# Attention scores of two heads: one zero-padded matmul over the whole array, or two on halves of its rows

## The chip, the cores and the metric

The kernel runs on one core of a Trainium2 chip. The metric is the device time of one execution in microseconds (us); the median of three runs of the kernel before is 1846.34 us (1845.67 to 1846.72). The engines are TensorE (PE in the rows, PEld its weight loads), VectorE (DVE), ScalarE (ACT), GpSimd (POOL) and SyncE (SP), which issues the transfers.

## The reference

Attention over pooled keys and values feeds two layers of matmuls. Batch 8, 8 heads, 576 positions, head size 64; keys and values are averaged over 8 positions, so each head has 72 keys.

```python
k_p = k.reshape(B, H, Sp, pool, D).mean(axis=3)        # 72 keys of 64
v_p = v.reshape(B, H, Sp, pool, D).mean(axis=3)
scores = scale * np.matmul(q, k_p.transpose(0, 1, 3, 2))
scores = scores - np.max(scores, axis=-1, keepdims=True)
attn = np.exp(scores)
attn = attn / (np.sum(attn, axis=-1, keepdims=True) + 1e-09)
x = np.matmul(attn, v_p)                               # to 4608 x 512
h = x @ w_in;  g = h * sigmoid(1.702 * h);  x = g @ w_out      # 512 -> 2048 -> 512
a = x @ w_a;   b = x @ w_b;  out = (a * b) @ w_out2            # 512 -> 1536 -> 512
```

## The kernel before

The 4608 positions are 36 query tiles of 128 (`u`), and four query tiles are a block of 512 (`j`, nine blocks). A batch has 4.5 query tiles, so four of the 36 lie across two batches; `pieces(u)` cuts such a tile into two halves of 64 positions. The two big layers run in four passes over the blocks; each float32 operand is split into a high and a low part, and `mm3` makes three matmuls of 128x512 of each product (lines 130 to 132, and 415 to 417 for the last matmul). They are most of the work: some 7300 of the 8592 MATMULs in the trace.

The attention of later blocks is spread between the big matmuls of the first pass. A query tile goes through these steps:

- `stage_b1(u, half)`, once for each half of the heads: the scores of two pairs of heads into one bank `sc` of PSUM (line 224), the negated maximum of each row on VectorE (line 231), four exponentials with their sums on ScalarE (line 234).
- `stage_b2(u)`: normalises the weights `at` on VectorE (line 248).
- `stage_c(u)`: eight transposes of `at` through PE (`pt`, line 256), copied to `aT` by ScalarE.
- `stage_d(u)`: attention times values, two heads into the two halves of the partitions of `px` (line 269), then the split into `xhi` and `xlo`.

A pair of heads stands in one `q` tile: 64 rows for the first head, 64 for the second. The keys stand in `kbd`, 128 rows and, for each pair, 144 columns: the first head's keys in rows 0 to 63 and columns 0 to 71, the second's in rows 64 to 127 and columns 72 to 143, zeros elsewhere (GpSimd, line 160). One matmul of 128 rows and 144 columns then gives the scores of both heads side by side. `sum_k` sums the raw keys on VectorE, and `to_kbd` scales them into place with two ScalarE instructions (lines 191 and 192).

PSUM has eight banks here: four in the pool `acc` for the sums of the big layers, and four in the pool `ps`, which `h`, `ab`, `sc`, `pt` and `px` share. The order on each engine is made by a scheduler that takes the code's order as its input; `spread` puts each attention step behind a step of the big layers, and `in_order` holds the steps of the start behind the newest VectorE instruction. In the trace a float32 matmul of the code is two MATMULs, each with its own weight load; a matmul whose output goes to 64 partitions of PSUM takes half of the array's columns (`px`, and `sc` of the four tiles across two batches).

Of the kernel before, what the change touches and what calls it, by code (L numbers as in the profile page):

```python
# [9 lines left out]
F32 = mybir.dt.float32  # L10
# [14 lines left out]
def tile_kernel(ctx, tc, q, k, v, w_in, w_out, w_a, w_b, w_o2, out):  # L25
# [13 lines left out]
    nc = tc.nc  # L39
    P = 128  # L40
    NU, _, NP, _ = q.shape
    B, SP, H, D, _ = v.shape
# [19 lines left out]
    ps = ctx.enter_context(tc.tile_pool(name="ps", bufs=4, space=bass.MemoryType.PSUM))  # L62
# [7 lines left out]
    def vec(made):  # L70
        newest[0] = made.ins
        return made
# [82 lines left out]

    at = ExitStack()
    ap_ = at.enter_context(tc.tile_pool(name="ap", bufs=1))
    kbd = [ap_.tile([P, NP, 2 * SP], F32, name=f"kbd{i}") for i in range(2)]
    for t in kbd:
        nc.gpsimd.memset(t, 0.0)  # L160

    q_t, ks_t, vs_t, at_t, atT_t, kraw_t, vraw_t = {}, {}, {}, {}, {}, {}, {}

    def pieces(u):

        done = 0
        while done < P:
            b, s = divmod(u * P + done, S)
            n = min(P - done, S - s)
            yield done, n, b  # L170
            done += n

    def load_q(u, t=None):
        q_t[u] = ap_.tile([P, NP, P], F32, tag="q", name="q", bufs=2) if t is None else t
        nc.sync.dma_start(out=q_t[u], in_=q[u])
# [8 lines left out]

    scale = 1.0 / (POOL * D ** 0.5)

    def to_kbd(b, half, ks):


        cs = slice(2 * half, 2 * half + 2)  # L190
        nc.scalar.mul(out=kbd[b % 2][0:D, cs, 0:SP], in_=ks[0:D], mul=scale)
        nc.scalar.mul(out=kbd[b % 2][D:P, cs, SP:2 * SP], in_=ks[D:P], mul=scale)

    def sum_k(b, half):
        ks = ap_.tile([P, 2, SP], F32, tag="ks", name="ks", bufs=1)
        raw = kraw_t.pop((b, half)).rearrange("p c (s r) -> p c s r", r=POOL)
        vec(nc.vector.tensor_reduce(out=ks, in_=raw, op=ALU.add, axis=AX.X))
        to_kbd(b, half, ks)

    def load_v(b, h, n, raw=None):  # L200
        if raw is None:
# [9 lines left out]
    def stage_b1(u, half):  # L211
        qT = q_t[u]
        if half == 0:
            at_t[u] = (
                ap_.tile([P, H, SP], F32, tag="at", name="at", bufs=2),
                ap_.tile([P, H], F32, tag="mx", name="mx", bufs=2),
                ap_.tile([P, H], F32, tag="sm", name="sm", bufs=2),
            )
        a, mx, sm = at_t[u]
        sc = ps.tile([P, H // 2, SP], F32, tag="ps", name="sc")  # L220
        for c in range(2):
            pair = 2 * half + c
            for o, n, b in pieces(u):
                nc.tensor.matmul(  # L224
                    out=sc[o:o + n, 2 * c:2 * c + 2, :].rearrange("p h k -> p (h k)"),
                    lhsT=qT[:, pair, o:o + n],
                    rhs=kbd[b % 2][:, pair, :],
                    start=True, stop=True,
                )
        hs = slice(half * (H // 2), (half + 1) * (H // 2))  # L230
        vec(nc.vector.tensor_reduce(out=mx[:, hs], in_=sc, op=ALU.max, axis=AX.X, negate=True))
        for c in range(H // 2):
            h = half * (H // 2) + c
            nc.scalar.activation(
                out=a[:, h, :], in_=sc[:, c, :], func=AF.Exp, bias=mx[:, h:h + 1],
                accum_out=sm[:, h:h + 1],
            )
        if half == 1:
            q_t.pop(u)
            if UB <= u + 2 < NU:  # L240
                load_q(u + 2)

# [43 lines left out]
    def slot(t, lo, hi):  # L286

        todo = [
            (t, op(stage_b1, t, 0)), (t - 1, op(stage_b2, t - 1)), (t - 2, op(stage_d, t - 2)),
            (t, op(stage_b1, t, 1)), (t - 1, op(stage_c, t - 1)),  # L290
        ]
        return [o for u, o in todo if lo <= u < hi]
# [4 lines left out]
    for b in range(2, B):  # L297
        u0 = b * S // P
        for t, ops in (
            (u0 - 5, [op(load_k, b, 0)]), (u0 - 4, [op(sum_k, b, 0), op(load_k, b, 1), op(load_v, b, 0, V)]),  # L300
            (u0 - 3, [op(sum_k, b, 1), op(load_v, b, V, V)]),
            (u0 - 2, [op(sum_v, b, 0, V), op(load_v, b, 2 * V, V)]),
            (u0 - 1, [op(sum_v, b, V, V), op(load_v, b, 3 * V, V)]),
            (u0, [op(sum_v, b, 2 * V, V)]), (u0 + 1, [op(sum_v, b, 3 * V, V)]),
        ):
            later[t] += ops
# [189 lines left out]
    for i in range(1, 4):  # L496
        fs = passes[i][1]
        for j in range(NB):
            n = place[i, j, fs[0]]
# [74 lines left out]
    def b1(u):  # L574
        return [op(stage_b1, u, half) for half in range(2)]
# [7 lines left out]

    c0, c1 = make_parts((1, 0)), make_parts((1, 1))
    in_order(op(sum_k, 0, 0), op(sum_k, 0, 1), b1(0)[0], c0[0], b1(0)[1], b1(1)[0], c0[1], b1(1)[1])
    in_order(op(sum_v, 0, 0, half_v), b2(0), op(sum_v, 0, half_v, half_v), b2(1), *b1(2))
    in_order(c0[2], cd(0), b1(3)[0], c0[3], cd(1), b1(3)[1], b2(2), c1[0], b2(3), c1[1], cd(2), c1[2], cd(3), c1[3])
# [5 lines left out]
    hs = {}  # L593
# [87 lines left out]
```

## Time and profile before

| | |
|---|---|
| median of three runs | 1846.34 us |
| the profiled execution | 1848.59 us |
| its span, first to last instruction | 1846.8 us |
| mean granted TensorE clock | 0.986 |
| busy: PE, VectorE, ScalarE | 1807.4, 843.7, 549.4 us |
| score MATMULs, busy | 320, 55.3 us (40.4 + 8.3 + 6.6) |
| `px` MATMULs, busy | 640, 45.5 us (40.4 + 5.1) |

Busy times of PE are unions over overlapping instructions: a MATMUL's listed duration runs to the modelled end of its last column, while the next has long begun. What one costs in a stream is therefore the step from its start to the next start, which the timeline gives. The attention ends at about 436 us; after that PE runs the big layers alone.

### The profile page before, as it was taken

What the parts mean: (1) busy time and instruction counts of PE and PEld (TensorE: products, weight loads), DVE (VectorE), ACT (ScalarE), POOL (GpSimd) and SP (SyncE); (2) the same over time, 40 slices, a digit from 0 to 9 for tenths busy, and PEclk for the clock granted to TensorE, in tenths of its full rate; (3) what the DMA queues carried; (4) which work ended last, traced back from release to release, by engine and by line L of the source; (5) the groups of instructions that cost most, each with busy time, mean ns of one, the idle gap of its engine ahead of it and who ended that gap; (6) DMA issues with size and microseconds to landing.
All of it is one profiled execution on the core that took longest, in us unless ns stands there. A gap on an engine that the chain in (4) does not pass through costs nothing.

```text
span 1846.8 us, 21557 instructions
## 1 busy us (share of the span) xinstructions
PE 1807.4 (98%) x8592; PEld 1487.3 (81%) x8592; DVE 843.7 (46%) x1440; ACT 549.4 (30%) x1373; POOL 1.7 (0%) x8
## 2 busy tenths in 40 slices
PE   5799999999999999999999999999999999999998
PEld 4668888888888888888888888888888888888887
DVE  6886767655744444445444445456212221221222
ACT  5555555553322222223222222222111111111111
POOL 0000000000000000000000000000000000000000
PEclk7899999999999999999999999999999999999999
DMA  9263454325333222333223433432211210220200
GB/s 295 105 215 140 170 162 145 128 80 196 147 114 126 91 103 83 123 126 137 103 92 137 171 125 121 153 114 92 91 39 53 92 68 24 92 91 12 80 24 23
DMA packets 58613, 206.92 MB, mean 112 GB/s; under 512 B 6576, under 2 KB 6576, under 8 KB 46704
## 3 DMA queue, kind: packets, MB, share of 16 engines
q1 hardware_dynamic: 58512, 205.55, 31.4%
q8 instruction: 67, 1.10, 0.2%
q14 instruction: 34, 0.28, 0.0%
HBM read 139.46 MB, written 66.06 MB: 111 GB/s over the span
## 4 chain that ended last, share of the span: by engine, by line
PE 95%; DVE 3%; ACT 1%; DMA 1%; issue 0%; DVEq 0%; ACTq 0%
PE ab L130 11%; PE ab L131 11%; PE ab L132 11%; PE h L130 7%; PE h L131 7%; PE h L132 7%; PE acc L130 7%; PE acc L131 7%; PE acc L132 7%; PE acc L415 5%; PE acc L416 5%; PE acc L417 5%; PE px L269 2%; PE sc L224 2%; PE pt L256 2%; DVE vs L209 1%
## 5 line engine op out<-in xcount | busy, mean ns | idle before, releaser
L130 PE MATMUL ab<-xhi,w 128*128 128x512 f32 x864 | 336.1, 389 | 0.0
L131 PE MATMUL ab<-xlo,w 128*128 128x512 f32 x864 | 336.1, 389 | 0.0
L132 PE MATMUL ab<-xhi,w 128*128 128x512 f32 x864 | 336.1, 389 | 0.0
L403 DVE TENSOR_TENSOR c<-c,ab 128x512 f32<-128x512 f32 x108 | 74.3, 688 | 529.5 <-PE ab L132 526.7
L130 PE MATMUL h<-xhi,w 128*128 128x512 f32 x576 | 227.5, 396 | 0.7 <-ACT xhi L85 0.7
L131 PE MATMUL acc<-glo,w 128*128 128x512 f32 x576 | 227.2, 394 | 0.0
L131 PE MATMUL h<-xlo,w 128*128 128x512 f32 x576 | 226.4, 393 | 0.0
L132 PE MATMUL h<-xhi,w 128*128 128x512 f32 x576 | 226.2, 393 | 0.0
L132 PE MATMUL acc<-ghi,w 128*128 128x512 f32 x576 | 225.0, 391 | 0.0
L375 DVE SCALAR_TENSOR_TENSOR g<-g,h 128x512 f32<-128x512 f32 x144 | 98.6, 685 | 232.7 <-ACT g L372 232.2
L130 PE MATMUL acc<-ghi,w 128*128 128x512 f32 x576 | 188.7, 400 | 2.8 <-ACT ghi L376 1.9
L132 PEld LDWEIGHTS ab<-xhi,w 128*128 128x128 f32 x864 | 162.2, 188 | 33.8
L130 PEld LDWEIGHTS ab<-xhi,w 128*128 128x128 f32 x864 | 162.2, 188 | 33.7
L131 PEld LDWEIGHTS ab<-xlo,w 128*128 128x128 f32 x864 | 162.2, 188 | 33.6
L372 ACT ACTIVATE g<-h 128x512 f32<-128x512 f32 x144 | 86.1, 598 | 339.8 <-PE h L132 330.0
L402 ACT COPY c<-ab 128x512 f32<-128x512 f32 x108 | 63.6, 589 | 356.9 <-PE ab L132 356.9
L415 PE MATMUL acc<-w,chi 128*128 128x512 f32 x432 | 168.0, 389 | 0.0
L416 PE MATMUL acc<-w,chi 128*128 128x512 f32 x432 | 168.0, 389 | 0.0
L417 PE MATMUL acc<-w,clo 128*128 128x512 f32 x432 | 167.6, 389 | 0.0
L85 ACT CAST chi<-c 128x512 fp32r<-128x512 f32 x108 | 66.9, 620 | 288.8 <-DVE c L403 288.8
L130 PEld LDWEIGHTS h<-xhi,w 128*128 128x128 f32 x576 | 109.4, 190 | 24.1 <-ACT xhi L85 1.1
L131 PEld LDWEIGHTS h<-xlo,w 128*128 128x128 f32 x576 | 109.6, 190 | 23.4 <-issue 0.4
(61 smaller groups left out, 2067.7 us busy)
## 6 DMA issues: line engine op xcount, KB each, us to landing
part<-ys SPq DMA_DIRECT2D x72, 256.0 KB
part<-part SPq DMA_DIRECT2D x18, 1024.0 KB
xhi<-yd SPq DMA_DIRECT2D x18, 1024.0 KB
xlo<-yd SPq DMA_DIRECT2D x18, 1024.0 KB
xd<-xhi SPq DMA_DIRECT2D x9, 1024.0 KB
xd<-xlo SPq DMA_DIRECT2D x9, 1024.0 KB
xhi<-xd SPq DMA_DIRECT2D x9, 1024.0 KB
xlo<-xd SPq DMA_DIRECT2D x9, 1024.0 KB
```

The source lines that it names most:

```text
L85: nc.scalar.copy(out=hi, in_=src)
L130: nc.tensor.matmul(out=o, lhsT=whi, rhs=xhi, start=first, stop=False)
L131: nc.tensor.matmul(out=o, lhsT=whi, rhs=xlo, start=False, stop=False)
L132: nc.tensor.matmul(out=o, lhsT=wlo, rhs=xhi, start=False, stop=last)
L224: nc.tensor.matmul(out=sc[o:o + n, 2 * c:2 * c + 2, :].rearrange("p h k -> p (h k)"), lhsT=qT[:, pair, o:o + n], rhs=kbd[b % 2][:, pair, : ...
L372: nc.scalar.activation(out=g, in_=hps, func=AF.Tanh, scale=0.5 * 1.702)
L375: made = vec(nc.vector.scalar_tensor_tensor(out=g, in0=g, scalar=1.0, in1=hps, op0=ALU.add, op1=ALU.mult))
L402: nc.scalar.copy(out=cc, in_=pab[0])
L403: made = nc.vector.tensor_tensor(out=cc, in0=cc, in1=pab[1], op=ALU.mult)
L415: nc.tensor.matmul(out=o, lhsT=chi[:, cs], rhs=whi, start=first, stop=False)
L416: nc.tensor.matmul(out=o, lhsT=chi[:, cs], rhs=wlo, start=False, stop=False)
L417: nc.tensor.matmul(out=o, lhsT=clo[:, cs], rhs=whi, start=False, stop=last)
```

## The change

The keys lose their zeros: `kT` holds 128 rows and 72 columns for each pair, the first head's keys in rows 0 to 63, the second's in rows 64 to 127, in the same columns. One ScalarE instruction of 128 rows writes what two of 64 rows did, and GpSimd's zero fill goes. The scores of a pair are two matmuls of 64 rows and 72 columns: one reads rows 0 to 63 of `q` and `kT`, the other rows 64 to 127. They go into two banks: `sc_t[u][0]` takes the even heads and `sc_t[u][1]` the odd ones. All scores of a query tile are now made in `stage_b1(u, 0)`, so both banks are taken there; the second call works on the second bank. A call's maximum and four exponentials are for every second head.

```diff
-    kbd = [ap_.tile([P, NP, 2 * SP], F32, name=f"kbd{i}") for i in range(2)]
-    for t in kbd:
-        nc.gpsimd.memset(t, 0.0)
+    kT = [ap_.tile([P, NP, SP], F32, name=f"kT{i}") for i in range(2)]
...
-    def to_kbd(b, half, ks):
-        cs = slice(2 * half, 2 * half + 2)
-        nc.scalar.mul(out=kbd[b % 2][0:D, cs, 0:SP], in_=ks[0:D], mul=scale)
-        nc.scalar.mul(out=kbd[b % 2][D:P, cs, SP:2 * SP], in_=ks[D:P], mul=scale)
+    def to_kT(b, half, ks):
+        nc.scalar.mul(out=kT[b % 2][:, 2 * half:2 * half + 2, :], in_=ks, mul=scale)
...
+            sc_t[u] = [ps.tile([P, H // 2, SP], F32, tag="ps", name="sc") for _ in range(2)]
+            for pair in range(NP):
+                for o, n, b in pieces(u):
+                    for e in range(2):
+                        r = slice(e * D, (e + 1) * D)
+                        nc.tensor.matmul(
+                            out=sc_t[u][e][o:o + n, pair, :], lhsT=qT[r, pair, o:o + n],
+                            rhs=kT[b % 2][r, pair, :], start=True, stop=True,
+                        )
         a, mx, sm = at_t[u]
-        sc = ps.tile([P, H // 2, SP], F32, tag="ps", name="sc")
-        for c in range(2):
-            pair = 2 * half + c
-            for o, n, b in pieces(u):
-                nc.tensor.matmul(
-                    out=sc[o:o + n, 2 * c:2 * c + 2, :].rearrange("p h k -> p (h k)"),
-                    lhsT=qT[:, pair, o:o + n],
-                    rhs=kbd[b % 2][:, pair, :],
-                    start=True, stop=True,
-                )
-        hs = slice(half * (H // 2), (half + 1) * (H // 2))
+        sc = sc_t[u][half]
+        hs = slice(half, H, 2)
...
-            h = half * (H // 2) + c
+            h = 2 * c + half
...
+            sc_t.pop(u)
```

The scheduler sets the instructions in another order. On PE, at the query tile whose scores stand ahead of `px` behind the 288th big matmul, there stood before (names end in a buffer's number; a row's end is the shape of the output's partitions and columns, and how many matmuls of the code stand in a row):

```order
L130 MATMUL h_1420<-xhi_1013,w_180 128x512
L131 MATMUL h_1420<-xlo_1014,w_180 128x512
L132 MATMUL h_1420<-xhi_1013,w_180 128x512
L224 MATMUL sc_1443<-kbd1_123,q_1256 128x144 x2
L269 MATMUL px_1456<-aT_1382,vs_728 64x128 x8
L224 MATMUL sc_1467<-kbd1_123,q_1256 128x144 x2
L130 MATMUL acc_1117<-ghi_1364,w_874 128x512
```

and now stands:

```order
L130 MATMUL h_1474<-xhi_1055,w_183 128x512
L131 MATMUL h_1474<-xlo_1056,w_183 128x512
L132 MATMUL h_1474<-xhi_1055,w_183 128x512
L222 MATMUL sc_1497<-kT1_123,q_1302 128x72 x4
L222 MATMUL sc_1498<-kT1_123,q_1302 128x72 x4
L268 MATMUL px_1517<-aT_1436,vs_756 64x128 x8
L130 MATMUL acc_1162<-ghi_1423,w_910 128x512
```

Eight score matmuls stand ahead of `px` where two stood ahead and two behind, and here the scheduler put the four of the first half of the rows (`sc_1497`) ahead of the four of the second. In other tiles it kept the code's order, the two banks in turn: of the 22 tiles within one batch from the 145th big matmul on, 11 stand so, four as here, two with three of one half ahead, one in turn but cut into five and three, and four cut in the middle. Such a cut, behind the 528th big matmul, where before there stood on PE

```order
L256 MATMUL pt_2201<-ident_78,at_2001 72x128 x4
L130 MATMUL acc_2015<-ghi_2125,w_580 128x512
L130 MATMUL acc_2016<-ghi_2125,w_580 128x512
L131 MATMUL acc_2015<-glo_2126,w_580 128x512
L132 MATMUL acc_2015<-ghi_2125,w_580 128x512
L131 MATMUL acc_2016<-glo_2126,w_580 128x512
L256 MATMUL pt_2207<-ident_78,at_2001 72x128 x4
L224 MATMUL sc_2220<-kbd0_122,q_2070 128x144 x2
L132 MATMUL acc_2016<-ghi_2125,w_580 128x512
```

now reads:

```order
L255 MATMUL pt_2279<-ident_78,at_2072 72x128 x4
L130 MATMUL acc_2093<-ghi_2199,w_608 128x512
L255 MATMUL pt_2285<-ident_78,at_2072 72x128 x4
L222 MATMUL sc_2298<-kT0_122,q_2145 128x72 x4
L131 MATMUL acc_2093<-glo_2200,w_608 128x512
L132 MATMUL acc_2093<-ghi_2199,w_608 128x512
```

Here the four matmuls of one half (`sc_2298`) stand alone between big matmuls, and those of the other half (`sc_2299`, four in a row as well) eleven big matmuls later. On ScalarE, at the very start of the program, there stood before

```order
L191 ACT_TABLE_LOAD
L191 ACTIVATE kbd_122<-ks 64x2x72
L192 ACTIVATE kbd_122<-ks 64x2x72
L191 ACTIVATE kbd_122<-ks 64x2x72
L192 ACTIVATE kbd_122<-ks 64x2x72
L234 ACTIVATE at,sm<-sc,mx 128x72 x4
L108 ACTIVATE tmp<-raw 128x512
```

and now

```order
L188 ACT_TABLE_LOAD
L188 ACTIVATE kT_122<-ks 128x144 x2
L108 ACTIVATE tmp<-raw 128x512
L232 ACTIVATE at,sm<-sc,mx 128x72 x4
L119 CAST w<-tmp 128x512
L232 ACTIVATE at,sm<-sc,mx 128x72 x8
```

Two scalings stand where four stood, and the first step of a weight's conversion (line 108) has moved ahead of the first four exponentials. Later in the program the exponentials of a query tile mostly stand eight in a row where they stood four and four.

## Rows read from the trace of the kernel before

**Rows 1.** Page: busy us (share of the span) per engine; shares of the last chain.
```profile
PE 1807.4 (98%) x8592; PEld 1487.3 (81%) x8592; DVE 843.7 (46%) x1440; ACT 549.4 (30%) x1373; POOL 1.7 (0%) x8
...
PE 95%; DVE 3%; ACT 1%; DMA 1%; issue 0%; DVEq 0%; ACTq 0%
```
**Rows 2.** Windows: stretch, length, busy us per engine, granted clock, DMA share, GB/s.
```profile
50.00:100.00 50.00, 38.18 (x235) 29.59 (x233) 45.12 (x79) 32.16 (x125) 0.00 (x0) 0.86 0.28 94
107.00:440.00 333.00, 332.10 (x2014) 271.28 (x2013) 222.54 (x401) 181.05 (x635) 0.00 (x0) 1.00 0.43 146
440.00:1846.00 1406.00, 1401.66 (x6184) 1160.28 (x6182) 534.44 (x889) 306.96 (x509) 0.00 (x0) 1.00 0.27 97
```
**Rows 3.** Waits of PE (us, times, longest): the run's longest; the one from 107 us.
```profile
PE pt L256 <- DVE at L248: 16.8, 5, 5.5
...
PE acc L130 <- ACT ys L433: 0.9, 1, 0.9
```
**Rows 4.** Timeline of PE, 423 to 427 us: start us, length us, instructions and count.
```profile
423.69 0.39 PE L132 MATMUL h<-xhi,w 128*128 128x512 f32 x1
...
424.37 0.39 PE L132 MATMUL h<-xhi,w 128*128 128x512 f32 x1
424.69 1.09 PE L269 MATMUL px<-aT,vs 72*64 72x128 f32 x16
...
426.05 0.40 PE L132 MATMUL acc<-ghi,w 128*128 128x512 f32 x1
```
**Rows 5.** Timeline of PE, scores between big matmuls, 113 to 115 us.
```profile
113.66 0.39 PE L132 MATMUL h<-xhi,w 128*128 128x512 f32 x1
113.88 0.65 PE L224 MATMUL sc<-kbd,q 128*128 128x144 f32 x4
...
114.60 0.39 PE L130 MATMUL h<-xhi,w 128*128 128x512 f32 x1
```
**Rows 6.** Timeline of PE, four transposes, and `px` of a tile across batches.
```profile
121.70 0.60 PE L256 MATMUL pt<-ident,at 128*72 128x128 f32 x4
...
282.32 1.20 PE L269 MATMUL px<-aT,vs 72*64 72x64 f32 x32
```
**Rows 7.** By tile (`sc`, `px`, `pt`): count: shortest/median/longest ns, first and last start us.
```profile
L224 PEld LDWEIGHTS sc<-kbd,q x288: 132/188/337, 43.9 to 417.1; 128*128 128x128 f32 x112, 128*64 128x64 f32 x32
...
L269 PEld LDWEIGHTS px<-aT,vs x640: 132/137/232, 22.9 to 434.8; 72*64 72x64 f32 x160
L269 PE MATMUL px<-aT,vs x640: 221/273/477, 22.9 to 434.9; 72*64 72x128 f32 x128, 72*64 72x64 f32 x32
...
L256 PE MATMUL pt<-ident,at x288: 270/273/428, 21.1 to 431.1; 128*72 128x128 f32 x144
```
**Rows 8.** Timeline of weight loads, the first two big ones behind a `px` group.
```profile
155.12 0.19 PEld L131 LDWEIGHTS acc<-glo,w 128*128 128x128 f32 x1 [0.17 <-issue]
155.23 0.19 PEld L132 LDWEIGHTS acc<-ghi,w 128*128 128x128 f32 x1
```
**Rows 9.** Timeline of PE, scores on halves of columns and `px`, 153 to 156 us.
```profile
153.29 0.39 PE L132 MATMUL h<-xhi,w 128*128 128x512 f32 x1
153.61 0.71 PE L224 MATMUL sc<-kbd,q 128*64 128x144 f32 x8
154.15 1.04 PE L269 MATMUL px<-aT,vs 72*64 72x128 f32 x16
...
155.46 0.39 PE L132 MATMUL acc<-ghi,w 128*128 128x512 f32 x1
```
**Rows 10.** Groups of ScalarE instructions: count | busy us, mean ns | idle before.
```profile
L191 ACT ACTIVATE kbd<-ks 64x144 f32<-64x144 f32 x16 | 5.2, 323 | 5.2 <-DVE ks L197 4.7 <-PE sc L224 0.3
L192 ACT ACTIVATE kbd<-ks 64x144 f32<-64x144 f32 x16 | 5.1, 320 | 0.2
```
**Rows 11.** Timeline of VectorE at the start: the second sum of keys.
```profile
8.54 1.35 DVE L197 TENSOR_REDUCE ks<-kvraw 128x144 f32<-128x1152 f32 x1 [2.06 <-ACT kbd L192]
```
**Rows 12.** Chain in order of time: start us, length us; eight exponentials with eight sums.
```profile
24.68 2.54 ACT at L234 x16
```

More of the change, by code (lines that the diff above doesn't have):

```diff
@@ L157, in tile_kernel @@
     ap_ = at.enter_context(tc.tile_pool(name="ap", bufs=1))
-    kbd = [ap_.tile([P, NP, 2 * SP], F32, name=f"kbd{i}") for i in range(2)]
-    for t in kbd:
-        nc.gpsimd.memset(t, 0.0)
-    q_t, ks_t, vs_t, at_t, atT_t, kraw_t, vraw_t = {}, {}, {}, {}, {}, {}, {}
+    kT = [ap_.tile([P, NP, SP], F32, name=f"kT{i}") for i in range(2)]
+    q_t, sc_t, vs_t, at_t, atT_t, kraw_t, vraw_t = {}, {}, {}, {}, {}, {}, {}
     def pieces(u):
@@ L197, in sum_k @@
         vec(nc.vector.tensor_reduce(out=ks, in_=raw, op=ALU.add, axis=AX.X))
-        to_kbd(b, half, ks)
+        to_kT(b, half, ks)
     def load_v(b, h, n, raw=None):
```

## The prediction

> **What bounds the kernel now.** The page's shares come first: TensorE (PE) is busy 98% of the span and makes 95% of the chain that ended last [rows 1]. Then the windows, since a share is an average over stages: from 107 to 440 us, where scores and attention are still computed between the big matmuls, PE is busy 332.1 of 333 us at a granted clock of 1.00, and to the end 1401.7 of 1406 [rows 2]. The waits say the same: from 107 us on PE waited 0.9 us in all [rows 3]. So from there on every PE nanosecond that is added or saved moves the end one for one, and VectorE and ScalarE, at 67% and 54%, have room. Before 107 us it is otherwise: PE waited 16.8 us for the normalised `at` of VectorE alone, and the granted clock from 50 to 100 us is 0.86 [rows 2, 3]. What PE gains or loses there mostly ends in such waits.
>
> The times are sums of start-to-start steps in the timeline, since the listed durations overlap. The big matmuls (128x512) step by (424.37 - 423.69) / 3 = 0.227 us [rows 4].
>
> **Prices of a score matmul.** *Before.* One float32 matmul of the code is two MATMULs of the trace. Four of 144 columns on the whole array make the second big matmul after them start 0.94 us after the one before (113.66 to 114.60): 0.94 less 2 x 0.227 is 0.49, or 0.122 each [rows 5]; 128 columns (`pt`) take (0.60 - 0.273) / 3 = 0.109 [rows 6, 7]. So a pair of heads costs 2 x 0.122 = 0.244 and a query tile (four pairs) 0.98.
>
> *Two tiles of the array at once.* The trace has no halves of rows, but halves of columns, in `px` and in the scores of query tiles that lie across two batches. There 16 `px` MATMULs of 128 columns take 8 steps, not 16: their whole group is 1.09 long with 0.273 for one, which leaves 0.82 for 7 steps and the load that stands open at the entry [rows 4, 7]. I take it that halves of rows run side by side too.
>
> *Which of load and matmul sets the step.* 72 columns alone would need 0.122 x 72 / 144 = 0.061. But each MATMUL has its own weight load, and that goes by the columns of the weights, which stay 128: two loads of 128 columns that stand back to back start 0.11 apart (155.12, 155.23; with one more digit 0.107), and the medians 188 and 137 ns for 128 and 64 columns differ by 51 ns for 64 columns [rows 7, 8]. Today a load hides behind 144 columns of matmul; behind 72 it cannot. The nearest row where a load is as long as its matmul is `px` with 64 columns of either: 32 MATMULs in 1.20 us, so (1.20 - 0.22 - 0.05) / 15 = 0.062 for a step of 0.053 of load, some 0.006 to 0.009 over it [rows 6, 7]. So I take 0.113 for a pair step. Its bounds: 0.065, if loads of half the rows did not hold it up, and 0.226, if the halves did not overlap. A query tile has 8 pair steps: 0.90 instead of 0.98. That is the whole gain per tile, 0.08 us.
>
> *Going to tiles and back.* A lone visit of 16 `px` between big matmuls takes 424.37 to 426.05, 1.68 us; less 2 x 0.227 and 8 x 0.109 it leaves 0.354 for changing the array over and back [rows 4]. The entry shows as 0.32 where 0.227 is normal, 0.09, and then the 0.05 load of 64 columns stands open; the way back costs about 0.10 and the open load of 128 columns, 0.11. So 0.145 into a form with 64-column weights, 0.20 into the whole array, and 0.20 into halves of rows, whose weights have 128 columns. Visits shared by scores and `px` (153.29 to 155.46: 2.17, less 0.454, 4 x 0.122 and 8 x 0.109, leaves 0.356) pay once, since both are halves of columns [rows 9]. Halves of rows and halves of columns are different forms: between them I charge 0.145 as well.
>
> **The sum after 107 us**, counted along the order of PE from the 145th big matmul on. Before: 90 whole matmuls x 0.244 = 22.0 and 24 on column halves, two at a time, 12 x 0.244 = 2.9, together 24.9 us; 34 visits x (0.145 + 0.20) = 11.7. After: 22 query tiles on row halves. In 17 of them all eight matmuls stand in one visit, 17 x 0.90 = 15.4; in four the scheduler put four of one half, then big matmuls, then four of the other, so that nothing runs beside them: 4 x 16 x 0.113 = 7.2; one stands as five and three, 10 x 0.113 = 1.1. Three tiles across two batches become quarters of the array, 32 steps x 0.065 = 2.1. Together 25.8, or +0.9. The visits: 27 entries into row halves x 0.20 = 5.4, 15 into column halves or quarters x 0.145 = 2.2, 16 changes between tiled forms x 0.145 = 2.3, 42 ways back x 0.20 = 8.4, together 18.3, or +6.6. Sum: **+7.5 us**. What was a plain part of the whole-array stream becomes 27 visits, and 0.08 us saved on a tile does not pay for 0.40.
>
> **The rest of the change.** The zero fill of `kbd` (two memsets on GpSimd) goes, and of the two ScalarE scalings per half batch, 323 and 320 ns, one stays [rows 10]: 16 x 0.32 = 5 us off ScalarE, which waits for others all the time, so nothing after 107 us. At the start it frees `ks` 0.33 us sooner, for which VectorE waited 2.06 us [rows 11], and the weight cast's first step (L108) now stands ahead of the first exponentials, not behind them; against that the first maximum needs both halves of the keys, no longer one. I take -0.5 for the start and +1 for the first ten query tiles at their higher PE price, most of it swallowed by waits for VectorE: +0.5, between -4 and +6, since the clock's low stretches before 107 us lie where PE waits, and their place can shift. Maxima and exponentials keep number and size.
>
> Forecast: 1846.34 + 7.5 + 0.5 = **1854.3 us**. The profiled execution took 1848.59 us with a span of 1846.8, 2.3 over the median: prices come from it, and the difference is carried over to the median, which the sum starts from.
>
> **Rivals.**
> *A, the halves do not overlap.* For it: no row has two row halves, and their loads may have to take turns. Against: loads and matmuls of column halves start side by side. Then 22 x 16 x 0.113 = 39.8 and 48 x 0.065 = 3.1 for the quarters: 42.9 instead of 24.9, +18, with the visits +24.6: 1871. It decides from a pair step of about 0.2.
> *B, the order within the tile counts.* In six of the 17 whole tiles the scheduler put three or four matmuls of one half ahead of those of the other. If MATMULs start strictly in order, those cost up to 0.8 us more: +4.5, 1859. Against it: the 64-column `px` stand two and two in the order (two of one half, two of the other, four MATMULs each), and in strict order would need 3 steps for 4; at 0.062 for a pair they ran as if free to pass each other [rows 6]. The Trainium skill states the strict order: "TensorE: Matmul & The Clock Gate", "Part 3: Packing small matmuls", has matmuls start and end in program order with no reordering. By it those `px` would take 24 steps, some 1.5 us, where the trace has 1.20, so I side with the row, but eight in a line is more than it shows.
> *C, banks and bursts.* Both score banks of the four that `ps` has are held until the eight exponentials are through, 2.54 us for such a burst [rows 12] instead of half of it, and `px` follows at once in 14 visits. If the next `h` or `pt` waits for a bank, or a cast of `ghi` for the burst, by 0.6 us at half of the 26 tiles that are left, it is some +8 on top: 1862. Against: PE waited 0.9 us so far [rows 3], and on ScalarE the burst mostly stands before `g`, not between `g` and `ghi`.
> *D, the faster side: the load does not hold.* With 0.065 a step the scores after take 17 x 0.52 + 4 x 1.04 + 0.65 + 2.1 = 15.8 instead of 24.9, -9.1, and the visits +6.6: -2.5, 1844; were entering and leaving row halves free as well, -10.5: 1836. The equal step of load and matmul in the 64-column `px` speaks against the first, the 0.354 of every visit against the second. The Trainium skill, "TensorEngine Tiling (Array Packing)", "Theoretical Speedup", gives up to 2x where the contraction is 64 or less; that is D's 0.061 a step, and no run here shows it.
>
> **How the numbers follow.** Forecast 42%, B 14%, A 14%, C 10%, D with paid visits 12%, D with free visits 5%, a start that comes out better by over 4 us (with the forecast's other terms halved) 3%. No change that a measurement of this kernel can tell means within 0.2%, 3.7 us: 1842.6 to 1850.0. Under it are D with free visits, the better start and a part of D: 12%. Within it are most of D and the forecast's low tail: 19%. Over it the rest: 69%. The range reaches from D at 1843 to just over A at 1872.
>
> **What would show it.** In the profile after: score MATMULs in pairs that start almost together, pair steps of 0.11 us (0.06: D; 0.22: A); about 27 more spots where the big matmul behind the scores starts 0.11 late; PE busy to the same 99% from 107 us, its waits under 2 us (else C); the halves of a four-and-four tile in 0.9 us (1.7: B). The forecast is wrong if the change of form costs nothing, or if 128-column loads of half the rows take half the time.

## The result, and the profile after

The kernel after takes 1857.23 us (median of four, 1856.34 to 1859.11), the kernel before 1846.41: a ratio of 1.006 with a 95% interval of 1.0048 to 1.0072, so 10.8 us slower. Its profiled execution has a span of 1857.2 us. The page's busy times and chain, to be read beside [rows 1]:

```profile
PE 1823.7 (98%) x8912; PEld 1499.1 (81%) x8912; DVE 842.7 (45%) x1440; ACT 542.7 (29%) x1357; POOL 0.7 (0%) x6
...
PE 95%; DVE 2%; DMA 1%; ACT 1%; issue 0%; SPq 0%; DVEq 0%; ACTq 0%
```

PE has 320 more MATMULs and is busy 16 us longer; ScalarE is busy 6.7 us less, and the end does not notice. The windows, beside [rows 2], and the waits of PE from 107 us on, beside [rows 3]:

```profile
50.00:107.00 57.00, 46.54 (x301) 36.57 (x300) 49.69 (x87) 32.35 (x123) 0.00 (x0) 0.77 0.32 101
107.00:440.00 333.00, 332.67 (x2196) 268.44 (x2195) 220.55 (x403) 175.55 (x629) 0.00 (x0) 1.00 0.41 138
440.00:1857.00 1417.00, 1412.10 (x6245) 1169.25 (x6243) 538.26 (x895) 309.93 (x515) 0.00 (x0) 1.00 0.27 99
```

```profile
PE h L130 <- ACT at L232: 0.3, 1, 0.3
```

From 107 us PE is as full as before and waits 0.3 us in all, at a granted clock of 1.00 (2.4 GHz). Whatever is lost there is work that PE got.

A visit of scores and `px` between big matmuls with the two banks in turn (start us, length us, instructions and count):

```profile
192.66 0.39 PE L132 MATMUL h<-xhi,w 128*128 128x512 f32 x1
192.97 1.12 PE L222 MATMUL sc<-kT,q 64*128 64x72 f32 x16
194.02 1.09 PE L268 MATMUL px<-aT,vs 72*64 72x128 f32 x16
195.04 0.50 PE L130 MATMUL acc<-ghi,w 128*128 128x512 f32 x1
195.38 0.39 PE L131 MATMUL acc<-glo,w 128*128 128x512 f32 x1
```

The 16 score MATMULs take 1.05 us from their first start to that of `px`. They start in pairs, the two of a pair 6 to 8 ns apart; the first step from pair to pair is 0.167 us, the other six are 0.111 to 0.113. The entry shows as 0.31 (192.66 to 192.97) and the way back as 0.34 (195.04 to 195.38), where 0.227 is normal. From start to second big matmul behind the visit it is 2.72; less 2 x 0.227 that leaves 2.27 for two forms, 8 x 0.112 of it for scores and 8 x 0.109 for `px`, so 0.50 for going in, changing and going back (the long first step counted there). A tile whose scores stand alone, 419.68 to 421.38:

```profile
419.68 0.39 PE L132 MATMUL h<-xhi,w 128*128 128x512 f32 x1
420.00 1.12 PE L222 MATMUL sc<-kT,q 64*128 64x72 f32 x16
421.05 0.50 PE L130 MATMUL acc<-ghi,w 128*128 128x512 f32 x1
421.38 0.39 PE L131 MATMUL acc<-glo,w 128*128 128x512 f32 x1
```

1.70 less 0.454 is 1.25 us for a whole query tile: 0.90 for its pairs and 0.35 for the visit. Before, the same scores took 0.98 as part of the whole-array stream [rows 5].

**Where the loss arises.** One trace of each kernel would have misled here, so each was traced three times (the further runs are below). The big matmuls are numbered as PE runs them; in the first trace of the kernel before the 145th starts at 122.1 us. Starts are those of the timeline; the recorded expectations below count them from a zero some 0.2 us later. Each entry is a start, or a difference of two starts, in the three traces:

| us | before | after | difference of means |
|---|---|---|---|
| start of the 25th | 54.0, 54.1, 54.3 | 54.0, 51.9, 54.7 | -0.6 |
| 25th to 97th | 54.0, 53.6, 52.4 | 56.2, 55.5, 56.3 | +2.7 |
| 97th to 145th | 14.1, 14.1, 14.4 | 15.5, 15.5, 15.5 | +1.3 |
| 145th to 1141st | 313.1, 312.1, 312.1 | 319.8, 319.4, 319.7 | +7.2 |
| 1141st to the end | the same | the same | 0 |

Together +10.6, beside +10.8 of the medians. Where PE is full the stretch repeats to 0.5 us in the kernel after; in the kernel before one trace has 1.0 more, of which 0.9 is the wait of [rows 3], so the loss there is 7.2 to 7.5. The scatter of the kernel after sits ahead of the 25th big matmul, that of the kernel before between the 25th and the 97th.

### The profile page after: what moved, and what is told of

Its sections match the earlier page's. It is cut to its first block, busy times and chain, and to the rows that moved or that the text cites. A ratio compares the mean times of both kernels' runs of the same rounds, so it can differ in the third digit from the quotient of the medians.

```text
span 1857.2 us, 22171 instructions
## 1 busy us (share of the span) xinstructions
PE 1823.7 (98%) x8912; PEld 1499.1 (81%) x8912; DVE 842.7 (45%) x1440; ACT 542.7 (29%) x1357; POOL 0.7 (0%) x6
## 4 chain that ended last, share of the span: by engine, by line
PE 95%; DVE 2%; DMA 1%; ACT 1%; issue 0%; SPq 0%; DVEq 0%; ACTq 0%
PE ab L131 11%; PE ab L132 11%; PE ab L130 11%; PE acc L130 7%; PE h L130 7%; PE h L131 7%; PE acc L131 7%; PE h L132 7%; PE acc L132 7%; PE acc L415 5%; PE acc L414 5%; PE acc L416 5%; PE sc L222 2%; PE px L268 2%; PE pt L255 2%; DMA raw<-in_moe_w_in_dram 1%
## 5 line engine op out<-in xcount | busy, mean ns | idle before, releaser
L132 PE MATMUL acc<-ghi,w 128*128 128x512 f32 x576 | 225.9, 392 | 0.0
L130 PE MATMUL acc<-ghi,w 128*128 128x512 f32 x576 | 193.1, 402 | 3.3 <-ACT ghi L375 3.3
L130 PEld LDWEIGHTS acc<-ghi,w 128*128 128x128 f32 x576 | 108.8, 190 | 27.8 <-ACT ghi L375 3.7
```

The source lines that it names most:

```text
L130: nc.tensor.matmul(out=o, lhsT=whi, rhs=xhi, start=first, stop=False)
L132: nc.tensor.matmul(out=o, lhsT=wlo, rhs=xhi, start=False, stop=last)
```

## The experiments

**Both matmuls of a pair on one half of the rows.** In the kernel after both read the first half of the rows, so that they cannot overlap; the second head's scores are left out:

```diff
-                        r = slice(e * D, (e + 1) * D)
+                        r = slice(0, D)
```

> Kernel after, but both matmuls of a pair read rows 0 to 63 of q and keys (the second head's scores are the first's again: the output is not the reference's); all counts, columns, banks and visits stay. Theory (row halves run side by side, 8 steps of 0.107 us a tile): nothing can overlap any more, 16 steps; from 107 us on +0.86 on each of 11 tiles in turn, +0.3 to 0.6 on seven others, +0.5 on the three in quarters, some 14 us, and 1 to 3 more before: 1871 to 1874. Rival (halves never overlapped): no change from after, 1857.

Measured: 1876.85 us (1876.26 to 1878.37), ratio 1.0166 (1.0151 to 1.0181). Two rows of its timeline, of the same kind of visit as at 192.97:

```profile
197.90 2.00 PE L222 MATMUL sc<-kT,q 64*128 64x72 f32 x16
199.83 1.09 PE L268 MATMUL px<-aT,vs 72*64 72x128 f32 x16
```

1.93 us where the kernel after has 1.05: 8 more steps of 0.11. So the halves of the rows do run side by side in the kernel after, and that alone is worth 0.88 us a tile there. The time is some 3 us over what was expected: from the 145th to the 1141st big matmul 335.4 us pass, 15.8 more than in the kernel after where some 14 were expected, and the 145th comes at 128.2 us, later than in any trace of the kernel after.

**72 columns without the tiles.** Zero-padded keys again, but each head by a matmul of its own, 128 rows and 72 columns on the whole array, into the two banks of the kernel after:

```diff
-                            out=sc_t[u][e][o:o + n, pair, :], lhsT=qT[r, pair, o:o + n],
-                            rhs=kT[b % 2][r, pair, :], start=True, stop=True,
+                            out=sc_t[u][e][o:o + n, pair, :], lhsT=qT[:, pair, o:o + n],
+                            rhs=kbd[b % 2][:, pair, e * SP:(e + 1) * SP], start=True, stop=True,
```

> Kernel after with the zero-padded keys back and one matmul per head of 128 rows and 72 columns on the whole array, into the same two banks, all scores at once: no visit for the scores of tiles within a batch. Theory (a MATMUL cannot step faster than the load of its 128 weight columns, 0.107 us): 16 x 0.107 = 1.71 us a tile where the kernel before has 0.98, +13 us from 107 us on: 1859 to 1863. Rival (72 columns cost half of 144, the loss of after is in the visits alone): 16 x 0.061 = 0.98, 1845 to 1848.

Measured: 1869.94 us (1867.96 to 1870.53), ratio 1.0128 (1.0111 to 1.0145). The rows:

```profile
196.46 0.39 PE L132 MATMUL h<-xhi,w 128*128 128x512 f32 x1
196.68 1.90 PE L225 MATMUL sc<-kbd,q 128*128 128x72 f32 x16
198.51 1.09 PE L271 MATMUL px<-aT,vs 72*64 72x128 f32 x16
```

There is no entry to pay (0.22 from the big matmul to the scores), and 16 MATMULs of 72 columns take 1.79 us with nothing else in the visit, 0.112 each; four of 144 columns take 0.122 each [rows 5]. Half the columns save 0.01 us: the step is set by the weight load of 128 columns. That is the theory's mechanism; its time is missed by some 7 us. From the 145th to the 1141st big matmul 327.9 us pass, 15.5 more than in the kernel before, and the 145th comes at 126.6 us, 4.9 late: the first ten tiles cost here too.

**Two banks at once, nothing else.** The kernel before with all four matmuls of a tile in `stage_b1(u, 0)` and both banks taken there:

```diff
+            sc_t[u] = [ps.tile([P, H // 2, SP], F32, tag="ps", name="sc") for _ in range(2)]
+            for pair in range(NP):
+                c = pair % 2
...
+                        out=sc_t[u][pair // 2][o:o + n, 2 * c:2 * c + 2, :].rearrange("p h k -> p (h k)"),
...
+        sc = sc_t[u][half]
```

> Kernel before, one part alone: all eight... that is, the four matmuls of 128 rows and 144 columns of a query tile are made at once, into two banks, as in after; maxima and exponentials by halves of the heads as before. Theory (two banks held and eight exponentials in a row cost PE nothing): 1843 to 1847, a little under before where two visits become one. Rival (banks and bursts make part of the loss): PE waits of several us from 107 us on, 1850 to 1855.

Measured: 1846.94 us (1844.77 to 1848.62), ratio 1.0001 (0.9991 to 1.001). Holding two banks and running the exponentials eight in a row costs nothing that can be measured. C falls. Its trace shows more. From 107 us on PE waits once:

```profile
PE acc L130 <- DVE ys L437: 1.5, 1, 1.5
```

Even so 310.6 us pass from the 145th to the 1141st big matmul, 1.5 to 2.5 less than in the kernel before: with the scores of a tile in one place PE enters a tiled form 29 times there, not 34. Beside this run, which gathers the scores as the kernel after does, the row halves cost 9 us in this stretch. Ahead of it the run loses: the 145th starts at 122.9 us, and from the 25th to the 97th it takes 54.7.

**Quarters.** The kernel after with every query tile cut into pieces of 64 positions, so that each score matmul takes 64 rows and 64 columns of the array and loads 64 columns of weights:

```diff
+    def quarters(u):
+        for o, n, b in pieces(u):
+            for s in range(o, o + n, D):
+                yield s, D, b
...
-                for o, n, b in pieces(u):
+                for o, n, b in quarters(u):
```

> Kernel after with every query tile cut into two pieces of 64 positions, as the four tiles across batches are: matmuls of 64 rows, 64 weight columns and 72 columns on quarters of the array. Theory (the load by weight columns sets the step): the load falls to 0.053 and a step of four to 0.066, so a tile takes 0.53 us of steps instead of 0.86, and the 64-column entry saves 0.05 a visit: 1839 to 1845, faster than before. Rival (what costs is the change of form, not the load): 22 tiles x 0 saved, 1854 to 1858.

Measured: 1844.03 us (1842.59 to 1845.48), ratio 0.9987 (0.9978 to 0.9997). The visit of scores and `px`:

```profile
140.66 0.39 PE L132 MATMUL h<-xhi,w 128*128 128x512 f32 x1
140.98 0.73 PE L228 MATMUL sc<-kT,q 64*64 64x72 f32 x32
141.64 1.09 PE L274 MATMUL px<-aT,vs 72*64 72x128 f32 x16
142.66 0.50 PE L130 MATMUL acc<-ghi,w 128*128 128x512 f32 x1
143.00 0.39 PE L131 MATMUL acc<-glo,w 128*128 128x512 f32 x1
```

Twice as many MATMULs take 0.66 us (140.98 to 141.64) where the row halves take 1.05. A tile whose scores stand alone takes 0.87 us with its visit, where the row halves take 1.25 and the kernel before 0.98. The number of columns in the weights, not the number of MATMULs, sets the price. From the 145th to the 1141st big matmul 309.5 us pass, 2.5 to 3.5 less than in the kernel before, but only 1.0 less than with the padded matmuls gathered in one place.

**Quarters with the order pinned.** The same, with each score matmul held behind the one before it, and the second half of the rows first:

```diff
+                        if last is None:
+                            last = score(pair, o, n, b, e).ins
+                        else:
+                            with tc.issue_after(last):
+                                last = score(pair, o, n, b, e).ins
```

> The quarters of 64 rows and 64 positions (the run with every tile cut into pieces of 64 positions), with the order of a tile's score matmuls pinned to the order of the code, the second half of the rows first. In the run of the quarters seven tiles stood with some matmuls of one quarter ahead. Theory: the look-ahead costs little where the step is 0.066 (at most 0.3 us a tile), and the pinned order cuts one matmul off the front of eight tiles, which then enter the tiled form twice, at 0.2 to 0.35 each: together within 2 us of the unpinned quarters, 1843 to 1846. Rival: as with the row halves the order costs 0.3 us or more in each of seven tiles and in the ten early ones, the cut matmuls little: 1840 to 1842.

Measured: 1843.7 us (1843.3 to 1846.66), ratio 0.9989 (0.998 to 0.9998): the same as without. Here one matmul of eight tiles stands in a visit of its own, 0.46 us each for two MATMULs, and PE waits 1.94 us once at 129 us; what the order gains beyond that is too small to be seen. Both are some 2.5 us faster than the kernel before, at the edge of what a measurement of this kernel can tell.

**One half of the rows first.** The kernel after with its loops in another order:

```diff
-            for pair in range(NP):
-                for o, n, b in pieces(u):
-                    for e in range(2):
+            for e in range(2):
+                for pair in range(NP):
+                    for o, n, b in pieces(u):
```

> The kernel after with the loop over the two halves of the rows outermost: the four score matmuls of one half are written ahead of the four of the other, in every query tile; from the 145th big matmul on, 17 whole tiles stand so (four in the kernel after), and four are cut between the halves, as there. Theory (look-ahead over weight loads is short): a tile in four-and-four takes 0.50 us more than one with the banks in turn, as 2.77 against 2.27 us in the kernel after with its px; 13 more such tiles, less the two with three ahead, make +6 to +6.5 us from 107 us on, and as many as 2 more in the ten tiles before that, at the lower clock: 1863 to 1866. Rival (matmuls on different halves pass each other freely, and the four slow places of the kernel after have another cause, such as what stands around them): 1855 to 1858. Second rival (strict order of starts): a four-and-four tile would take 0.75 us more (15 steps for 8 of 0.107), 1867 to 1871.

Measured: 1862.92 us (1862.44 to 1863.22), ratio 1.0088 (1.0074 to 1.0102). From the 145th to the 1141st big matmul 326.1 us pass, 6.4 more than in the kernel after, as the theory says. Every whole tile now looks like this:

```profile
143.98 0.39 PE L132 MATMUL h<-xhi,w 128*128 128x512 f32 x1
144.30 1.62 PE L222 MATMUL sc<-kT,q 64*128 64x72 f32 x16
145.84 1.09 PE L268 MATMUL px<-aT,vs 72*64 72x128 f32 x16
```

1.54 us instead of 1.05. The starts inside such a tile tell how. In the kernel after, at 320.83 us, the eight MATMULs of the first half start at 0, 0.17, 0.28, 0.39, 0.50, 0.61, 0.73 and 0.84 us; the first of the second half, ninth in the order, starts at 0.51, beside the fifth. The next seven follow by the same steps, to 1.34. So here a MATMUL passed three of the other half, the sixth to the eighth, and no more. In the two tiles with six MATMULs of one half ahead (three matmuls of the code) the other half starts 0.28 us in, beside the third: three passed again. Two windows of 0.45 us of the kernel after, one in turn and one of these, show how many have started:

```profile
192.97 0.67 PE L222 MATMUL sc<-kT,q 64*128 64x72 f32 x8
...
320.83 0.66 PE L222 MATMUL sc<-kT,q 64*128 64x72 f32 x4
```

**The first nine tiles as before.** The tiles of the first two batches use the zero-padded keys and the code of the kernel before (here `kbd` beside `kT`), all others the code of the kernel after:

```diff
+        if u < 9:
+            sc = ps.tile([P, H // 2, SP], F32, tag="ps", name="sc")
...
+                        rhs=kbd[b % 2][:, pair, :],
...
+        elif half == 0:
+            sc_t[u] = [ps.tile([P, H // 2, SP], F32, tag="ps", name="sc") for _ in range(2)]
```

> The nine query tiles of the first two batches are computed as in the kernel before (zero-padded keys, one matmul of 144 columns, a bank for each half of the heads), all later ones as in the kernel after. Theory: of the 11 us that the kernel after loses, 2 to 3 come from the nine first tiles, where PE waits for VectorE and ScalarE at a low clock (three four-and-four tiles of 2.8 to 2.9 us, and a weight cast of ScalarE that stands ahead of the first exponentials and waits for its transfer). Then the 145th big matmul begins within 1 us of where it does in the kernel before, not 3 us later, and the rest, in which the scheduler here cuts one tile more between big matmuls (some 1.7 us by the prices of the kernel after), makes +9 to +10: 1855 to 1857. Rival: the early 3 us are the scatter of single executions and of the clock's low stretches, all of the loss lies after 107 us: the 145th big matmul stands 2 to 4 us late again and the time is 1858 to 1860.

Measured: 1856.4 us (1854.96 to 1857.23), ratio 1.0051 (1.0038 to 1.0063). The 145th big matmul starts at 122.5 us, 0.5 behind the latest trace of the kernel before (121.0 to 122.1) and 2.5 earlier than the mean of the kernel after; from the 25th to the 97th it takes 52.6 us. From the 145th to the 1141st it takes 320.4, 0.7 more than the kernel after; one tile of scores more was expected to be cut there, but the trace shows none; it is the `px` of one tile that stands cut, into 14 and two MATMULs. Its window from 50 to 107 us:

```profile
50.00:107.00 57.00, 43.05 (x266) 33.77 (x265) 53.72 (x94) 35.81 (x135) 0.00 (x0) 0.85 0.39 122
```

PE is busy 3.5 us less there than in the kernel after, at a granted clock of 0.85 instead of 0.77. The three traces of the kernel before have 41.8 to 45.5 us at 0.79 to 0.88 there, those of the kernel after 46.5 to 46.7 at 0.77 to 0.79. The early loss is real, and it belongs to the way the first nine tiles' scores are made. This run gives them back the padded matmuls and the two calls at once. The run with two banks, padded matmuls in one call, lies between: 54.7 us from the 25th to the 97th, beside 52.4 to 54.0 in the kernel before and 55.5 to 56.3 in the kernel after. So a part of the early loss may come from gathering the scores, not from the row halves; one trace does not say how much.

**Both kernels again**, for further traces:

> The kernel before, unchanged, for a second trace of it: its profiled execution so far was 2.3 us over the median, and the loss of the kernel after is split by that one trace into 3.7 us before the 145th big matmul and 6.8 us from there to the last of the attention. Theory: the split is right within 1 us, so the 145th big matmul begins at 121 to 123 us here too, and the 1141st 312 to 314 us behind it. Rival: the 2.3 us lie behind the 145th, and the stretch there is 310 to 311 us.

> The kernel after, unchanged, for a second trace of it (the first was 1.9 us over the median). Theory: the 145th big matmul begins 2.5 to 4 us later than in the kernel before, as in the first trace (125.5 us), and the stretch to the 1141st takes 319 to 321 us. Rival: the late start was that execution's, and it begins at 122 to 124 us, as it did in the run with one half of the rows first (123.1 us) though more tiles stand in four-and-four there.

> The kernel before once more, for the scatter of the two stretches: theory and rival as for the second trace of it (145th big matmul at 121 to 123 us; 312 to 314 us from there to the 1141st, or 310 to 311).

> The kernel after once more, for the scatter of the two stretches: theory and rival as for the second trace of it (145th big matmul at 125 to 126 us, or 122 to 124; 319 to 321 us from there to the 1141st).

Measured: 1847.36 and 1846.58 us for the kernel before, 1855.86 and 1859.75 for the kernel after; the table above has their stretches. The kernel before holds both its starts, to 0.2 us, and its stretch (the theory, but for the 0.9 us wait). For the kernel after both sides were half right: the 145th big matmul starts at 125.7, 122.9 and 126.5 us, and the stretch is the theory's. ScalarE's row tells which is which. In the first, second and third trace of the kernel after, one after the other:

```profile
19.20 0.67 ACT L108 ACTIVATE tmp<-raw 128x512 f32<-128x512 f32 x1 [3.76 <-DMA raw<-in_moe_w_out_dram]
```

```profile
17.92 0.67 ACT L108 ACTIVATE tmp<-raw 128x512 f32<-128x512 f32 x1 [2.82 <-DMA raw<-in_moe_w_out_dram]
```

```profile
19.72 0.67 ACT L108 ACTIVATE tmp<-raw 128x512 f32<-128x512 f32 x1 [4.35 <-DMA raw<-in_moe_w_out_dram]
```

The scheduler put this weight step ahead of exponentials that could run, and it waits for the weight's transfer; the 25th big matmul starts at 54.0, 51.9 and 54.7 us, in the same order. In the kernel before the step's longest wait for that transfer was 0 to 1.9 us, and the 25th comes within 0.3 us in all three traces.

## Why the prediction was right, and where it was not

The side was right and the measured time lies in the range, 3 us over the forecast of 1854.3. By its steps:

- **What bounds.** Right: from 107 us on PE waits 0.3 us, and 5 us taken off ScalarE bring nothing. The scaling that stayed is one of 321 ns for 128 rows, where [rows 10] had two:

```profile
L188 ACT ACTIVATE kT<-ks 128x144 f32<-128x144 f32 x16 | 5.1, 321 | 10.1 <-DVE ks L193 10.1
```

- **The pair step.** Taken as 0.113, measured 0.112: the halves overlap, and the load of 128 columns sets the step. The runs with the same rows, with 72 columns on the whole array, and with quarters show both halves of the argument; A and D fall.
- **The visits.** Taken as 0.40 alone and 0.545 with `px`, measured 0.35 and 0.50: a load of 128 columns costs no more at the entry than one of 64, as the lone `px` visit of [rows 4] has 0.354 too. Over 27 visits that is 1.3 us too much. This is the term that decides the case, 0.08 us saved on a tile against 0.35, and here it held.
- **The order within the tile.** Charged nothing, which was wrong: the sum took a matmul as free to pass any number of others. By the prediction's own sign a four-and-four tile was to take 0.9 us, or 1.7 with B; it took 1.54. It costs 0.50 us more and one with three ahead 0.27; 4 x 0.50 and 2 x 0.27 make +2.5. B had the place right and the size wrong: by strict order it would be 7 x 0.112 = 0.78. The row against it, the 64-column `px`, has four MATMULs of one half ahead of the other's, so that the fifth has three to pass, just as many as were passed here; "eight in a line is more than it shows" was the weak spot. The Trainium skill ("TensorE: Matmul & The Clock Gate", "Part 3: Packing small matmuls") has matmuls start in program order. The trace disagrees, since the ninth starts beside the fifth; by that rule the run with one half first would have come to 1867 or more, and it took 1862.92.
- **The sum after the 145th big matmul.** Predicted +7.5, measured 7.2 to 7.5. It is partly luck: -1.3 and +2.5 for the two terms above would make 8.7, and what lies against it, 1.2 to 1.5, was not split.
- **The first ten tiles.** The mis-sized term: +1 for them and -0.5 for the start, where the start is -0.6 in the mean and the tiles +4.0. Of these, 1.3 lie between the 97th and the 145th big matmul, at a granted clock of 1.00 with PE full: the sum said that PE is the bound from 107 us but counted only from the 145th, at 122.1. There one tile of scores is cut into two visits of 1.24 us each (at 116.3 and 119.8 us), where the kernel before has 0.98 of scores in all. The other 2.7 lie before, where the sum expected PE's extra work to vanish in waits for VectorE. The wait that stands at 63 us did shrink, but the scores behind it run at the lower clock (granted 0.50 from 64.0 to 68.6 us, which is 1.2 GHz; steps doubled). The timeline of the kernel after:

```profile
63.94 1.90 PE L255 MATMUL pt<-ident,at 128*72 128x128 f32 x8 [4.59 <-DVE at L247]
65.77 2.91 PE L222 MATMUL sc<-kT,q 64*128 64x72 f32 x16
68.61 2.03 PE L268 MATMUL px<-aT,vs 72*64 72x64 f32 x32
70.56 2.08 PE L130 MATMUL acc<-ghi,w 128*128 128x512 f32 x4
```

and that of the kernel before at the same place:

```profile
63.04 1.89 PE L256 MATMUL pt<-ident,at 128*72 128x128 f32 x8 [5.55 <-DVE at L248]
64.73 1.27 PE L224 MATMUL sc<-kbd,q 128*128 128x144 f32 x4
65.93 1.26 PE L269 MATMUL px<-aT,vs 72*64 72x64 f32 x32
67.12 0.76 PE L224 MATMUL sc<-kbd,q 128*128 128x144 f32 x4
67.62 1.20 PE L130 MATMUL acc<-ghi,w 128*128 128x512 f32 x4
```

  The wait is 1.0 us shorter, and behind it the big matmuls start 2.9 us later (67.62, 70.56). In this trace of the kernel before the clock was back by the `px` group: 1.26 us, beside 1.20 in [rows 6]. After, the same group takes 2.03, and the four big matmuls behind it 2.08 instead of 1.20. But the low clock there is not by itself the loss: in the second trace of the kernel before it was still low in the same two rows,

```profile
66.09 2.03 PE L269 MATMUL px<-aT,vs 72*64 72x64 f32 x32
...
69.01 2.08 PE L130 MATMUL acc<-ghi,w 128*128 128x512 f32 x4
```

  and from the 25th to the 97th that trace took 53.6 us all the same. That the way the first nine tiles' scores are made costs the 2.7 is shown by the run that undoes it (52.6). How much of it is the row halves' longer work, how much the gathering in one call and how much the clock elsewhere was not told apart; the run with one half first, with more tiles in four-and-four, took 55.7 us from the 25th to the 97th, no more than the kernel after, so the four-and-four order is not the cause.
- **The start.** The second sum of keys waits 1.23 us instead of 2.06 [rows 11], and now for its transfer:

```profile
7.45 1.35 DVE L193 TENSOR_REDUCE ks<-kvraw 128x144 f32<-128x1152 f32 x1 [1.23 <-DMA kvraw<-in_k_dram]
```

  The sum counted 0.33 us for the scaling that is gone and missed the larger part. Before, ScalarE loaded its function table only when `ks` was there, ahead of the first scaling; after, it does so at the very start of the program, where it is in nobody's way:

```profile
6.56 1.28 ACT L191 ACT_TABLE_LOAD   x1 [6.56 <-DVE ks L197]
```

```profile
0.73 1.28 ACT L188 ACT_TABLE_LOAD   x1 [0.73 <-PEq L664]
```

  The first scaling starts 1.6 us sooner (7.86, 6.26). So -0.6 beside the -0.5 of the sum is luck. What was missed too is that the weight step, moved ahead, makes the start hang on a transfer: a scatter of 2.8 us at the 25th big matmul, where before it was 0.3.
- **Banks and bursts.** No price, as forecast: eight exponentials in a row [rows 12] are now the rule, and PE waited 0.3 us for one of them in all from 107 us on.

The Trainium skill ("TensorEngine Tiling (Array Packing)", "Theoretical Speedup") gives up to 2x for a contraction of 64. The runs agree for one and the same matmul: 1.79 us for 16 of 72 columns on the whole array, 0.90 for them on row halves. But the kernel before did not run that matmul; its one of 144 columns did both heads for 0.122 a MATMUL.

## What to carry to other kernels

Before splitting a matmul that is padded with zeros into two tiles of the array, price three things from a trace: the weight load, which goes by the columns of the weights and not by the columns moved; the step into and out of the tiled form, 0.35 us for each visit between whole-array matmuls; and the order, since matmuls of different tiles must stand close together to run side by side. Here 0.08 us saved on a tile met 0.35 for its visit; quarters, which halve the load as well, just about pay. A sum over a stream that bounds the kernel has to begin where the stream begins to bound, and work added before that is not hidden just because its engine waits there.

## What had not been expected of the hardware

- MATMULs on different row halves pass each other in the order, but only over a short distance: the second half began beside the fifth of eight, which makes 12 to 13 steps where 8 would do and 15 would be strict order. On quarters, with one half of the rows first, the cost of the order was 0.30 us a tile (2.19 against 1.89 with `px`).
- On the whole array a MATMUL of 72 columns steps by 0.112 us, one of 144 by 0.122, so that half the columns save next to nothing while the weights keep their 128.
- Two MATMULs alone in a visit of quarters cost 0.46 us, of which some 0.33 is the visit.
